# The gradient of wq in five separately placed pieces, and head groups of four whose out and dx products spread over 25 ticks

## The chip, the core and the metric

The kernel runs on one core of one Trainium2 chip. The metric is device time in microseconds (us) of one execution. The engines named here are TensorE (PE in the profile: matrix products and transposes; PEld is its weight load), VectorE (DVE), ScalarE (ACT), GpSimd (POOL) and SyncE (SP), whose queue issues all DMA transfers. PSUM is the memory that TensorE writes to; VectorE and ScalarE copy from there to SBUF, and such a copy is what "empties a bank" means below.

## What is computed

Two attention blocks, A and B, with the same shapes and separate data, forward and backward. Each has 8 batches, 32 heads, 96 queries per batch of width 640, and 512 cached keys and values of width 128 per batch and head. Everything is bfloat16 in memory.

```python
q = (x @ wq).reshape(B, Sq, H, Dh).transpose(0, 2, 1, 3)
scores = jnp.einsum("bhqd,bhkd->bhqk", q, k_cache) * (Dh ** -0.5)
p = _softmax(scores, axis=-1)
o = jnp.einsum("bhqk,bhkd->bhqd", p, v_cache)
out = o.transpose(0, 2, 1, 3).reshape(B, Sq, H * Dh) @ wo
```

The kernel returns `out` of both blocks side by side and, for a given gradient of it, the gradients of x, k_cache, v_cache, wq and wo: dx, dk, dv, dwq and dwo.

## The kernel before

**Ticks.** The work is cut into small functions. Each is handed to an `Emitter` with a tick and a slot number, and `run` sorts them by tick, then slot, then order of arrival, and calls them. So the order of each engine's instructions is written out by these numbers. Instructions of S and the softmax (`c_s2a` to `c_s3b`) have a raised priority and stand somewhat earlier than their slot says: S is placed into the last products of the tick before. One tick is the time that one pair (head, batch) takes; a head has 8 ticks, a block 256, and head h begins at tick `c0t = tick0 + 8 h`.

**Per pair.** One tick holds the stages of nine neighbouring pairs: S (L298, one product of 512 columns), its row maximum `negm` on VectorE (L300), the exponential `E_sb` on ScalarE (L310, with a read of the accumulated sums), `rinv` on VectorE (L320), `P_sb` on GpSimd (L329), the transposes of P and of dS on TensorE (L365, L346), their copies `PT_sb` (ScalarE, L378) and `dST_sb` (VectorE, L348), the products O and dQ (L359, L340, both into `x_ps`) with their copy `OD` (ScalarE, L375), dV (L389) and dK (L432) with copies on ScalarE (L392, L435), dP and its row correction dl (L417, L419), and `dS_sb` on VectorE (L421).

**Per head**, in slots behind the pair's work:
- `pB`, tick -3 of the head: transposes of wo and wq of the head, copies `woT_h` (ScalarE) and `wqT_h` (VectorE).
- `pC`, ticks -2 to 0: QT and dOT in two widths, 512 and 256 columns (L243).
- `pD`, ticks 1 and 2: the same two transposed back, copies `dOnat_h` and `Qnat_h` on VectorE.
- `qA`, tick 18: O transposed, copy `Onat` on ScalarE; tick 17: dQ transposed, copy `dQnat` on VectorE.
- `qB`, ticks 19 and 20: dwo in two halves of 320 columns (L469), copies on ScalarE and VectorE.
- `qD`, for odd heads: dwq of the pair of heads in 5 chunks of 128 rows, each six products of 256 columns (L490). Two chunks share a PSUM bank at tick 18, two at tick 19, one at tick 21; the copies are on VectorE (L162). The pair's store follows one tick after the last.

**Per group of heads.** The sums over heads in out and dx are taken in groups, held in float32 accumulators in SBUF. Block A has groups of 5, 5, 5, 5, 4, 4, 4 heads, block B of 5, 5, 5, 5, 5, 5, 2. For each group, `gU` runs 24 pieces: out and dx, six row tiles each, once with 512 and once with 128 columns; every piece is one product per head of the group into one bank (L514). The first group's banks are emptied by ScalarE, the others are added to the accumulators by VectorE (L518, L520). With `cLg` the tick of the group's last pair, a group of five puts its 12 out pieces on ticks cLg+7 to cLg+15 and its 12 dx pieces on cLg+16 to cLg+24; many ticks get two pieces, and 22 of 40 none. A group of four in block A takes seven ticks for each half.

**Buffers.** All PSUM tiles come from one ring of eight banks (`bank`). `wqT_h` has a ring of seven, `OD` (O and dQ of a head, read by `gU`) seven slots, `dQnat`, `dwq_sb`, `Onat` and `dwo_sb` one buffer each. A new `wqT_h` waits until the last dx piece of the group that read the old one.

Of the kernel before, what the change touches and what calls it, by code (L numbers as in the profile page):

```python
# [45 lines left out]
HK = dict(pA=-10, pA2=-9, pB=-3, pC0=[-2, 0], pC1=[-1, 0], pD1=1, pD0=2, qA0=18, qA1=17, qB=[19, 20], qD=[(18, 0, 2), (19, 2, 4), (21, 4, 5)])  # L46
EV = dict(pB0="act", pB1="dve", pC00="act", pC01="act", pC10="act", pC11="dve", pD0="dve", pD1="dve", qA0="act", qA1="dve", qB0="act", qB1="dve", qD="dve", gU="act")
GSPREAD0 = 9
PRIO_OFF = 2000
GSPREAD1 = 9  # L50
SLOTS = dict(LOAD=0, S2A=5, S2B=5.5, S1=6, S8=10, S7=20, S5=30, S4=40, S6=50, S3A=52, S3B=53, S5B=54, HEAD=SL_HEAD, GRP=SL_GRP)


def build_block(tc, em, tick0, blk, x, kc, vc, wq, wo, g_all, out_all, dx, dk, dv, dwq, dwo, ident, ones, pools, HG=6, first=True, groups=None):
    nc = tc.nc
    B, Sq, D = x.shape
    _, H, Sk, Dh = kc.shape
# [147 lines left out]
    def pB(h):  # L205
        def f():
            st = HS[(blk, h)]
            woT_ps = bank([128, DC * 128], BF16, "woT_ps")
            for c in range(DC):
                nc.tensor.transpose(woT_ps[:, c * 128:(c + 1) * 128], st["wo_h"][:, c * 128:(c + 1) * 128], ident[:])  # L210
            woT_h = hd.tile([128, DC * 128], BF16, name="woT_h", bufs=1)
            evac(EV["pB0"], woT_h[:], woT_ps[:])
            st["woT_h"] = woT_h
            wqT_ps = bank([128, DC * 128], BF16, "wqT_ps")
            for c in range(DC):
                nc.tensor.transpose(wqT_ps[:, c * 128:(c + 1) * 128], st["wq_h"][:, c, :], ident[:])
            wqT_h = hst.tile([128, D], BF16, name="wqT_h")
            evac(EV["pB1"], wqT_h[:], wqT_ps[:])
            st["wqT_h"] = wqT_h
            st["slot"] = (blk * H + h) % OD.shape[2]  # L220
            st["OT_h"] = OD[:, 0, st["slot"]]
            st["dQT_h"] = OD[:, 1, st["slot"]]
            st["QT_h"] = hd.tile([128, T], BF16, name="QT_h")
            st["dOT_h"] = hd.tile([128, T], BF16, name="dOT_h")
        return f

    def pC(h, which, si):
        def f():
# [12 lines left out]
            q_ps = bank([128, w], F32, "q_ps")  # L241
            for c in range(DC):
                nc.tensor.matmul(q_ps[:], lhs(c), rhsT[:, c, t0:t0 + w], start=(c == 0), stop=(c == DC - 1))  # L243
            evac(EV["pC%d%d" % (which, si)], dst[:, t0:t0 + w], q_ps[:], sc)
        return f
# [314 lines left out]
    for g in range(NG):  # L560
        h0 = GH0[g]
        for hh in range(groups[g]):
            h = h0 + hh
            c0t = tick0 + h * B
            if not (first and h == 0):
                em.add(c0t + HK["pA"], SLOTS["LOAD"] + 1.7, pA(h))
                em.add(c0t + HK["pA2"], SLOTS["LOAD"] + 1.7, pA2(h))
            em.add(c0t + HK["pB"], SL_HEAD, pB(h))
            fh = first and h == 0
            p0, p1, d1, d0, late = HK["pC0"], HK["pC1"], HK["pD1"], HK["pD0"], 0  # L570
            if fh:
                p1, d1, d0, late = [3, 3], 3, 4, 7
            elif h == 0:
                p0, p1, d1, d0, late = [-2, 2], [0, 3], 3, 4, 7
            for si in range(NTS):
                em.add(c0t + p0[min(si, 1)], SL_HEAD, pC(h, 0, si))
                em.add(c0t + p1[min(si, 1)], SL_HEAD + late, pC(h, 1, si))
            em.add(c0t + d1, SL_HEAD + (8 if late else 0), pD(h, 1))
            em.add(c0t + d0, SL_HEAD, pD(h, 0))
            for b in range(B):  # L580
                ct = c0t + b
                if b % NB == 0:
                    em.add(tick0 - 12 if first and h == 0 and b == 0 else ct + OFF["ldk"], SLOTS["LOAD"], c_ld(h, b, "K", 7))
                    em.add(ct + OFF["ldv"], SLOTS["LOAD"], c_ld(h, b, "V", 6))
                    if not k_on_pe(h, b):
                        em.add(ct + OFF["kt"], SLOTS["LOAD"] + 1, c_xt(h, b, "KT", 4))
                    em.add(ct + OFF["vt"], SLOTS["LOAD"] + 1, c_xt(h, b, "VT", 4))
                if k_on_pe(h, b):
                    em.add(ct + 2, SLOTS["S1"], c_s1(h, b))
# [29 lines left out]
        if g == 0:  # L619
            em.add(cLg + OFF["s5"] - 2, SL_LOAD, setup_acc)  # L620
        subs = [(0, t, gi) for t in range(TT) for gi in range(len(gsplits))] + [(1, t, gi) for t in range(TT) for gi in range(len(gsplits))]
        n_out = TT * len(gsplits)
        for i, (which, t, gi) in enumerate(subs):
            if which == 0:
                tk = cLg + OFF["s5"] + 2 + (i * gs0) // n_out
            else:
                tk = cLg + OFF["s8"] + 2 + gs0 - 3 + ((i - n_out) * gs1) // n_out
            em.add(tk, SL_GRP, gU(g, which, t, gi))
# [126 lines left out]
```

## Time and profile before

| | |
|---|---|
| runs | 1643.6, 1643.09, 1642.14 us; median 1643.09 |
| profiled execution | 1643.09 us, of which the profile's span is 1641.3 |
| granted TensorE clock | 1.000 |
| TensorE matmul, busy | 1621.3 us (99%) |
| TensorE weight load, busy | 1289.1 us (79%) |
| ScalarE, busy | 1388.7 us (85%) |
| VectorE, busy | 1268.2 us (77%) |
| GpSimd, busy | 526.7 us (32%) |
| DMA | 454.96 MB, mean 277 GB/s |

A matmul's record lasts longer than its share of the array: records of neighbouring matmuls overlap. So the busy share of TensorE says little on its waits. What a matmul costs in a stream is the distance from its start to the next one's. A timeline row with "x4" is four such instructions, merged, with the start of the first; text in brackets is idle time of the engine before it and what ended that.

### The profile page before, as it was taken

The page shows a single profiled execution, that of the slowest core. Times are in us where ns is not written, and L with a number is a line of the kernel's source. Part 1 is how long each engine was busy: PE and PEld are TensorE (multiplying, and loading weights), DVE is VectorE, ACT ScalarE, POOL GpSimd, SP SyncE. Part 2 cuts the span into 40 slices and gives each one's busy share as a digit, 9 for nine tenths or more (in the row PEclk, how much of TensorE's full clock was granted, in tenths as well). Part 3 has the DMA queues.
Part 4 walks back from the last instruction along what each step waited for, and adds up shares of the span by engine and source line. Part 5 has one row for each costly group of instructions (what it writes and reads, how often), then busy time and mean ns, then how long its engine had stood idle before and what let it go on. Part 6 is the DMA issues. An engine that isn't in the chain of part 4 may idle for free.

```text
span 1641.3 us, 55280 instructions
## 1 busy us (share of the span) xinstructions
PE 1621.3 (99%) x21048; PEld 1289.1 (79%) x21048; DVE 1268.2 (77%) x2856; ACT 1388.7 (85%) x3518; POOL 526.7 (32%) x1034
## 2 busy tenths in 40 slices
PE   8999999999999999999999999999999999999999
PEld 7887787787787787877878877877877877877876
DVE  6886677778787787788878867878778778777777
ACT  7999897898798797988869998978977978987975
POOL 2333232333233232333323332323322322332332
PEclk9999999999999999999999999999999999999999
DMA  9999999999999999999999999999999999999994
GB/s 266 289 282 294 269 291 291 271 271 292 260 272 293 279 274 271 264 281 285 297 284 292 293 289 279 284 298 260 291 291 258 280 277 282 283 292 259 281 276 146
DMA packets 875626, 454.96 MB, mean 277 GB/s; under 512 B 548192, under 2 KB 875360, under 8 KB 875360
## 3 DMA queue, kind: packets, MB, share of 16 engines
q1 hardware_dynamic: 875360, 451.43, 112.4%
q8 instruction: 165, 2.70, 0.7%
q14 instruction: 101, 0.83, 0.1%
HBM read 161.09 MB, written 159.12 MB: 195 GB/s over the span
## 4 chain that ended last, share of the span: by engine, by line
PE 81%; ACT 10%; DVE 4%; issue 3%; DMA 2%; SPq 0%; POOL 0%; ACTq 0%; DVEq 0%; POOLq 0%
PE q_ps L243 13%; PE o_ps L514 12%; PE dwq_ps L490 6%; PE dP_ps L417 6%; PE dK_ps L432 6%; PE dV_ps L389 5%; PE S_ps L298 5%; PE dst_ps L346 5%; PE dwo_ps L469 4%; PE x_ps L365 4%; PE x_ps L359 4%; PE x_ps L340 4%; ACT E_sb L310 3%; ACT dK_sb L435 2%; PE n_ps L258 2%
## 5 line engine op out<-in xcount | busy, mean ns | idle before, releaser
L329 POOL TENSOR_SCALAR P_sb<-E_sb,rinv 96x512 bf16<-96x512 bf16 x512 | 352.5, 689 | 1087.9 <-DVE rinv L320 1053.6
L310 ACT ACTIVATE E_sb<-S_ps,negm 96x512 bf16<-96x512 f32 x512 | 354.8, 693 | 119.2 <-DVE negm L300 116.8
L421 DVE SCALAR_TENSOR_TENSOR dS_sb<-dP_ps,dl_ps,P_sb 96x512 bf16<-96x512 f32 x512 | 383.6, 749 | 48.9 <-PE dl_ps L419 40.2
L435 ACT ACTIVATE dK_sb<-dK_ps 128x512 bf16<-128x512 f32 x512 | 306.9, 599 | 97.5 <-PE dK_ps L432 96.5
L300 DVE TENSOR_REDUCE negm<-S_ps 96x1 f32<-96x512 f32 x512 | 347.7, 679 | 44.3 <-PE S_ps L298 42.1
L392 ACT ACTIVATE dV_sb<-dV_ps 128x512 bf16<-128x512 f32 x512 | 315.8, 617 | 0.0
L378 ACT ACTIVATE PT_sb<-x_ps 128x384 bf16<-128x384 bf16 x512 | 257.5, 503 | 0.0
L514 PEld LDWEIGHTS <-OD 128*128 128x128 bf16 x1536 | 135.7, 98 | 103.3 <-issue 1.3
L389 PE MATMUL dV_ps<-dOnat_h,P_sb 96*128 96x128 bf16 x2048 | 197.9, 219 | 0.6 <-DVE dOnat_h L160 0.6
L432 PE MATMUL dK_ps<-Qnat_h,dS_sb 96*128 96x128 bf16 x2048 | 197.8, 219 | 0.0
L417 PE MATMUL dP_ps<-VT,dOT_h 128*96 128x512 bf16 x512 | 195.4, 382 | 0.7
L298 PE MATMUL S_ps<-KT,QT_h 128*96 128x512 bf16 x488 | 184.7, 379 | 3.9 <-ACT E_sb L310 2.7
L407 POOL TENSOR_TENSOR prod<-OD,dOT_h 128x96 bf16<-128x96 bf16 x512 | 185.6, 362 | 8.8 <-ACT OD L375 8.2
L348 DVE COPY dST_sb<-dst_ps 128x384 bf16<-128x384 bf16 x512 | 177.2, 346 | 14.0 <-PE dst_ps L346 13.2
L320 DVE RECIPROCAL rinv<-rowsum 96x1 f32<-96x1 f32 x512 | 80.0, 156 | 138.8 <-ACT E_sb L310 134.8
L346 PE MATMUL dst_ps<-ident,dS_sb 96*128 96x96 bf16 x2048 | 171.8, 206 | 4.3 <-ACT PT_sb L378 3.6
L375 ACT ACTIVATE OD<-x_ps 128x192 bf16<-128x192 f32 (+1 forms) x515 | 172.5, 335 | 3.4 <-PE x_ps L340 3.4
L359 PE MATMUL x_ps<-PT_sb,V_sb 128*128 128x96 bf16 x2048 | 172.2, 206 | 0.5 <-ACT PT_sb L378 0.5
L365 PE MATMUL x_ps<-ident,P_sb 96*128 96x96 bf16 x2048 | 171.7, 205 | 0.6 <-POOL P_sb L329 0.3
L340 PE MATMUL x_ps<-dST_sb,K_sb 128*128 128x96 bf16 x2048 | 170.7, 206 | 0.0
L340 PEld LDWEIGHTS <-K_sb 128*128 128x128 bf16 x2048 | 133.7, 98 | 37.1
L514 PE MATMUL o_ps<-wo_h,OD 128*128 128x128 bf16 (+1 forms) x768 | 141.0, 299 | 0.0
(75 smaller groups left out, 3051.9 us busy)
## 6 DMA issues: line engine op xcount, KB each, us to landing
out_dram<-dV_sb SPq DMA_DIRECT2D x256, 256.0 KB, 3.9
out_dram<-dK_sb SPq DMA_DIRECT2D x256, 256.0 KB, 3.6
K_sb<-in_A_k_cache_dram SPq DMA_DIRECT2D x128, 256.0 KB, 4.1
V_sb<-in_A_v_cache_dram SPq DMA_DIRECT2D x128, 256.0 KB, 4.1
K_sb<-in_B_k_cache_dram SPq DMA_DIRECT2D x128, 256.0 KB, 4.2
V_sb<-in_B_v_cache_dram SPq DMA_DIRECT2D x128, 256.0 KB, 4.0
out_dram<-dwo_sb SPq DMA_DIRECT2D x64, 160.0 KB, 3.2
out_dram<-dwq_sb SPq DMA_DIRECT2D x32, 320.0 KB, 3.8
```

Of the source, the lines that this page charges most:

```text
L298: nc.tensor.matmul(S_ps[:], hs["QT_h"][:, tok], st["KT"], start=True, stop=True)
L300: nc.vector.tensor_reduce(negm[:], S_ps[:], axis=AX.X, op=ALU.max, negate=True)
L310: nc.scalar.activation(E_sb[:], st["S_ps"][:], ACT.Exp, bias=st["negm"][:], scale=1.0, accum_out=rowsum[:])
L329: pinned(nc.gpsimd.tensor_scalar(P_sb[:], st["E_sb"][:], st["rinv"][:], 0.0, op0=ALU.mult, op1=ALU.add))
L340: nc.tensor.matmul(dQT_ps, st["K_sb"][:, c, :], st["dST_sb"][:, c * Sq:(c + 1) * Sq], start=(c == 0), stop=(c == KC - 1))
L389: nc.tensor.matmul(dV_ps[:, c * 128:(c + 1) * 128], P_sb[:, c * 128:(c + 1) * 128], hs["dOnat_h"][:, b * 128:(b + 1) * 128], start=True, s ...
L392: nc.scalar.activation(SB[(blk, h, b // 2, "v")][:, b % 2], dV_ps[:], ACT.Identity, scale=1.0)
L417: nc.tensor.matmul(dP_ps[:], hs["dOT_h"][:, tok], st["VT"], start=True, stop=True)
L421: nc.vector.scalar_tensor_tensor(dS_sb[:], dP_ps[:], dl_ps[:, 0:1], st["P_sb"][:], op0=ALU.subtract, op1=ALU.mult)
L432: nc.tensor.matmul(dK_ps[:, c * 128:(c + 1) * 128], dS_sb[:, c * 128:(c + 1) * 128], hs["Qnat_h"][:, b * 128:(b + 1) * 128], start=True, s ...
L435: nc.scalar.activation(SB[(blk, h, b // 2, "k")][:, b % 2], dK_ps[:], ACT.Identity, scale=1.0)
L514: nc.tensor.matmul(o_ps[:], src[:, t * 128:(t + 1) * 128], rhs, start=(hh == 0), stop=(hh == groups[g] - 1))
```

## The change

Four edits go together.

1. `Emitter.add` takes an estimate of the work's TensorE and ScalarE time in ns and keeps a load per tick, TensorE's minus 0.8 of ScalarE's. The calls for pB, pC, pD, qA, qB, gU and the K transposes of the first heads pass such numbers; the pair's own stages pass none.
2. `qD` of every odd head but the block's last is cut into five pieces of one chunk each. They are placed after everything else has been entered: each goes to the tick with the lowest load among ticks 18 to 29 of the odd head, at most two per tick; two in the same tick are emitted as one call with one bank. The last pair of heads of each block keeps the old ticks and pieces.
3. `qA` of dQ moves for even heads from tick 17 to tick 21, behind the other head work of its tick. Odd heads keep tick 17.
4. Block A has eight groups of 4, block B groups of 5, 5, 4, 4, 4, 4, 4, 2. A group of four puts its 12 out pieces on ticks cLg+7 to cLg+18, one each, and its 12 dx pieces on cLg+20 to cLg+31. Groups of five and two, and the last but one group of block B, keep nine, three and nine ticks for each half.

```diff
+HK = dict(pA=-10, ..., qA0=18, qA1=17, qA1e=21, qDw=(18, 29), qB=[19, 20], qD=[(18, 0, 2), (19, 2, 4), (21, 4, 5)])
...
-    def add(self, tick, slot, fn):
+    def add(self, tick, slot, fn, pe=0, act=0):
         self.items.append((tick, slot, self.n, fn))
         self.n += 1
+        self.load[tick] = self.load.get(tick, 0.0) + pe - ACT_SHARE * act
...
-            em.add(c0t + hk["qA1"], SL_HEAD, qA(h, 1))
-            for (k_, c_lo, c_hi) in hk["qD"]:
-                if c_lo < DC and h % 2 == 1:
-                    em.add(c0t + k_, SL_HEAD + 2, qD(h, c_lo, min(c_hi, DC)))
-            if h % 2 == 1:
+            em.add(c0t + (hk["qA1"] if h % 2 == 1 else HK["qA1e"]), SL_HEAD + (0 if h % 2 == 1 else 3), qA(h, 1), pe=335)
+            if h == H - 1:
+                for (k_, c_lo, c_hi) in hk["qD"]:
+                    em.add(c0t + k_, SL_HEAD + 2, qD(h, c_lo, min(c_hi, DC)), pe=655 * (c_hi - c_lo))
                 em.add(c0t + hk["qD"][-1][0] + 1, SLOTS["LOAD"] + 1.6, qD_st(h))
...
-        gs0 = max(3, (GSPREAD0 * groups[g]) // HG)
-        gs1 = max(3, (GSPREAD1 * groups[g]) // HG)
+        gs0, gs1 = {2: (3, 3), 4: (13, 13)}.get(groups[g], (9, 9))
...
+    for h in range(1, H - 1, 2):
+        c0t = tick0 + h * B
+        ticks = []
+        for _ in range(DC):
+            k_ = min((k for k in range(HK["qDw"][0], HK["qDw"][1] + 1) if ticks.count(k) < 2), key=lambda k: em.load.get(c0t + k, 0.0))
+            em.load[c0t + k_] = em.load.get(c0t + k_, 0.0) + 655
+            ticks.append(k_)
+        ticks.sort()
+        for k_ in sorted(set(ticks)):
+            em.add(c0t + k_, SL_HEAD + 2, qD(h, ticks.index(k_), ticks.index(k_) + ticks.count(k_)))
+        em.add(c0t + ticks[-1] + 1, SLOTS["LOAD"] + 1.6, qD_st(h))
...
-           ..., HG=5, ..., groupsA=None, groupsB=(5, 5, 5, 5, 5, 5, 2)):
+           ..., HG=5, ..., groupsA=(4,) * 8, groupsB=(5, 5, 4, 4, 4, 4, 4, 2)):
```

More of the change, by code (lines that the diff above doesn't have):

```diff
@@ L19, in __init__ @@
         self.n = 0
-    def add(self, tick, slot, fn):
+        self.load = {}
+    def add(self, tick, slot, fn, pe=0, act=0):
         self.items.append((tick, slot, self.n, fn))
         self.n += 1
+        self.load[tick] = self.load.get(tick, 0.0) + pe - ACT_SHARE * act
     def run(self):
@@ L45 @@
 OFF = dict(ldk=-5, ldv=-4, kt=-3, vt=0, s2=3, s3=3, s4=4, s5=5, s6=6, s7=7, s8=8)
-HK = dict(pA=-10, pA2=-9, pB=-3, pC0=[-2, 0], pC1=[-1, 0], pD1=1, pD0=2, qA0=18, qA1=17, qB=[19, 20], qD=[(18, 0, 2), (19, 2, 4), (21, 4, 5)])
+HK = dict(pA=-10, pA2=-9, pB=-3, pC0=[-2, 0], pC1=[-1, 0], pD1=1, pD0=2, qA0=18, qA1=17, qA1e=21, qDw=(18, 29), qB=[19, 20], qD=[(18, 0, 2), (19, 2, 4), (21, 4, 5)])
 EV = dict(pB0="act", pB1="dve", pC00="act", pC01="act", pC10="act", pC11="dve", pD0="dve", pD1="dve", qA0="act", qA1="dve", qB0="act", qB1="dve", qD="dve", gU="act")
 GSPREAD0 = 9
+ACT_SHARE = 0.8
 PRIO_OFF = 2000
@@ L567, in build_block @@
                 em.add(c0t + HK["pA2"], SLOTS["LOAD"] + 1.7, pA2(h))
-            em.add(c0t + HK["pB"], SL_HEAD, pB(h))
+            em.add(c0t + HK["pB"], SL_HEAD, pB(h), pe=558, act=713)
             fh = first and h == 0
@@ L575, in build_block @@
             for si in range(NTS):
[L576 to L579, printed above, removed]
+                em.add(c0t + p0[min(si, 1)], SL_HEAD, pC(h, 0, si), pe=1090 if si == 0 else 546, act=522 if si == 0 else 420)
+                em.add(c0t + p1[min(si, 1)], SL_HEAD + late, pC(h, 1, si), pe=1090 if si == 0 else 546, act=621 if si == 0 else 0)
+            em.add(c0t + d1, SL_HEAD + (8 if late else 0), pD(h, 1), pe=446)
+            em.add(c0t + d0, SL_HEAD, pD(h, 0), pe=446)
             for b in range(B):
@@ L588, in build_block @@
                 if k_on_pe(h, b):
-                    em.add(ct + 2, SLOTS["S1"], c_s1(h, b))
+                    em.add(ct + 2, SLOTS["S1"], c_s1(h, b), pe=223)
                 em.add(ct + OFF["s2"], SLOTS["S2A"], c_s2a(h, b))
@@ L603, in build_block @@
             hk = HK if first or h < H - 1 else dict(HK, qA0=13, qB=[14, 15], qA1=16, qD=[(19, 0, 2), (19, 2, 4), (19, 4, 5)])
-            em.add(c0t + hk["qA0"], SL_HEAD, qA(h, 0))
+            em.add(c0t + hk["qA0"], SL_HEAD, qA(h, 0), pe=335, act=820)
             for di in range(len(wsplits)):
-                em.add(c0t + hk["qB"][di], SL_HEAD + 1, qB(h, di))
+                em.add(c0t + hk["qB"][di], SL_HEAD + 1, qB(h, di), pe=815, act=443 if di == 0 else 0)
             em.add(c0t + hk["qB"][-1] + 1, SLOTS["LOAD"] + 1.6, qB_st(h))
-            em.add(c0t + hk["qA1"], SL_HEAD, qA(h, 1))
-            for (k_, c_lo, c_hi) in hk["qD"]:
-                if c_lo < DC and h % 2 == 1:
-                    em.add(c0t + k_, SL_HEAD + 2, qD(h, c_lo, min(c_hi, DC)))
-            if h % 2 == 1:
+            em.add(c0t + (hk["qA1"] if h % 2 == 1 else HK["qA1e"]), SL_HEAD + (0 if h % 2 == 1 else 3), qA(h, 1), pe=335)
+            if h == H - 1:
+                for (k_, c_lo, c_hi) in hk["qD"]:
+                    em.add(c0t + k_, SL_HEAD + 2, qD(h, c_lo, min(c_hi, DC)), pe=655 * (c_hi - c_lo))
                 em.add(c0t + hk["qD"][-1][0] + 1, SLOTS["LOAD"] + 1.6, qD_st(h))
         cLg = tick0 + (h0 + groups[g] - 1) * B + B - 1
-        gs0 = max(3, (GSPREAD0 * groups[g]) // HG)
-        gs1 = max(3, (GSPREAD1 * groups[g]) // HG)
+        gs0, gs1 = {2: (3, 3), 4: (13, 13)}.get(groups[g], (9, 9))
         if not first and g == NG - 2:
@@ L627, in build_block @@
                 tk = cLg + OFF["s8"] + 2 + gs0 - 3 + ((i - n_out) * gs1) // n_out
-            em.add(tk, SL_GRP, gU(g, which, t, gi))
+            em.add(tk, SL_GRP, gU(g, which, t, gi), pe=groups[g] * gsplits[gi][1] / 2.4, act=440 if g == 0 else 0)
             if g == NG - 1 and gi == len(gsplits) - 1:
                 em.add(tk + 1, SLOTS["LOAD"] + 1.6, gU_st(which, t))
+    for h in range(1, H - 1, 2):
[9 more added lines that the diff above has]
+        em.add(c0t + ticks[-1] + 1, SLOTS["LOAD"] + 1.6, qD_st(h))
     pools["c_s45"] = c_s45
```

2 lines of the change are left out of this document (1 added, 1 removed).

## The prediction

> **What bounds the kernel now.** I read the profile page first, then the matmuls in order of time, then ScalarE's and VectorE's rows in the same stretches.
>
> ```profile
> span 1641.3 us, 55280 instructions
> PE 1621.3 (99%) x21048; PEld 1289.1 (79%) x21048; DVE 1268.2 (77%) x2856; ACT 1388.7 (85%) x3518; POOL 526.7 (32%) x1034
> PE 81%; ACT 10%; DVE 4%; issue 3%; DMA 2%; SPq 0%; POOL 0%; ACTq 0%; DVEq 0%; POOLq 0%
> ```
>
> TensorE carries the run, but its 99% hides waits, since a matmul's record reaches into the next one's. Starts show them. The timeline of TensorE (start, duration, line, operation; in brackets a wait) has a light head:
>
> ```profile
> 23.50 0.34 PE L346 MATMUL dst_ps<-ident,dS_sb 96*128 96x96 bf16 x4
> ...
> 94.60 0.60 PE L243 MATMUL q_ps<-gT,woT_h 128*128 128x256 bf16 x4
> 95.04 0.33 PE L340 MATMUL x_ps<-dST_sb,K_sb 128*128 128x96 bf16 x4
> 95.21 0.34 PE L346 MATMUL dst_ps<-ident,dS_sb 96*128 96x96 bf16 x4
> 95.38 0.39 PE L432 MATMUL dK_ps<-Qnat_h,dS_sb 96*128 96x128 bf16 x4
> 95.61 0.34 PE L359 MATMUL x_ps<-PT_sb,V_sb 128*128 128x96 bf16 x4
> ...
> 96.17 0.38 PE L417 MATMUL dP_ps<-VT,dOT_h 128*96 128x512 bf16 x1
> 96.39 0.17 PE L419 MATMUL dl_ps<-ones,prod 128*96 128x1 bf16 x1
> ...
> 97.58 0.34 PE L346 MATMUL dst_ps<-ident,dS_sb 96*128 96x96 bf16 x4
> ...
> 100.15 0.34 PE L346 MATMUL dst_ps<-ident,dS_sb 96*128 96x96 bf16 x4
> ...
> 101.82 0.38 PE L298 MATMUL S_ps<-KT,QT_h 128*96 128x512 bf16 x1 [0.16 <-ACT E_sb L310]
> ...
> 102.88 0.34 PE L346 MATMUL dst_ps<-ident,dS_sb 96*128 96x96 bf16 x4
> ...
> 105.29 0.34 PE L346 MATMUL dst_ps<-ident,dS_sb 96*128 96x96 bf16 x4
> ...
> 107.27 0.33 PE L340 MATMUL x_ps<-dST_sb,K_sb 128*128 128x96 bf16 x4
> 107.77 0.33 PE L346 MATMUL dst_ps<-ident,dS_sb 96*128 96x96 bf16 x4 [0.17 <-ACT PT_sb L378]
> ...
> 1623.44 0.34 PE L346 MATMUL dst_ps<-ident,dS_sb 96*128 96x96 bf16 x4
> ```
>
> Unhindered, four matmuls of 96 columns start 0.17 us apart, four of 128 columns 0.23, one of 512 columns 0.22, four of 256 columns 0.44 (320 columns in proportion). One tick runs from a dst group to the next; there are 512 dst groups, the first at 23.50 and the last at 1623.44, so 511 ticks of 3.13 us on average. Priced by those distances, the matmuls between them need 3.06 us per tick. So all waits together are about 34 us: more than that the change can't win between these rows.
>
> Where are they? The ticks at 95.21 and 97.58 hold the same matmuls (nat and n transposes), yet last 2.37 and 2.57: 0.20 lost. Those at 100.15 and 102.88 both hold one dwo half: 2.73 against 2.41: 0.32 lost. At 107.27 the x group starts, dst should follow 0.17 later and follows after 0.50: 0.33 lost. ScalarE's timeline gives the reason:
>
> ```profile
> 99.80 0.60 ACT L392 ACTIVATE dV_sb<-dV_ps 128x512 bf16<-128x512 f32 x1
> 100.28 0.82 ACT L157 ACTIVATE Onat<-nat_ps 128x768 bf16<-128x768 bf16 x1
> 100.97 0.70 ACT L310 ACTIVATE E_sb<-S_ps,negm 96x512 bf16<-96x512 f32 x1
> ...
> 103.17 0.48 ACT L157 ACTIVATE dwo_sb<-dwo_ps 128x320 bf16<-128x320 f32 x1
> 103.48 0.74 ACT L310 ACTIVATE E_sb<-S_ps,negm 96x512 bf16<-96x512 f32 x1
> ```
>
> ScalarE needs 2.20 us for the six instructions of every tick (100.97 to 103.17), plus 0.69 for Onat and 0.31 for dwo. Two such ticks cost it 5.40 us, TensorE 2.37 + 2.41 = 4.78. In light ticks ScalarE is the bound, while TensorE leads it elsewhere. In the whole trace 18, 18 and 21 ticks have these three contents with neither dwq nor out/dx in them, and lose 0.20, 0.32 and 0.33 each with little scatter: 3.6 + 5.7 + 6.9 = 16.2 us.
>
> The second kind of wait sits in the heaviest ticks, where two out/dx pieces meet. VectorE and TensorE around one:
>
> ```profile
> 298.41 0.38 PE L417 MATMUL dP_ps<-VT,dOT_h 128*96 128x512 bf16 x1
> 298.86 0.75 DVE L421 SCALAR_TENSOR_TENSOR dS_sb<-dP_ps,dl_ps,P_sb 96x512 bf16<-96x512 f32 x1 [0.22 <-PE dl_ps L419]
> 299.54 0.54 DVE L160 COPY dQnat<-nat_ps 128x768 bf16<-128x768 bf16 x1
> 300.00 0.68 DVE L300 TENSOR_REDUCE negm<-S_ps 96x1 f32<-96x512 f32 x1
> 300.10 0.34 PE L346 MATMUL dst_ps<-ident,dS_sb 96*128 96x96 bf16 x4
> 300.60 0.68 DVE L160 COPY dOnat_h<-n_ps 96x1024 bf16<-96x1024 bf16 x1
> 301.33 0.12 PEld L417 LDWEIGHTS <-dOT_h 128*96 128x96 bf16 x1 [0.28 <-DVE dOnat_h L160]
> 304.27 0.34 PE L346 MATMUL dst_ps<-ident,dS_sb 96*128 96x96 bf16 x4
> ```
>
> dQnat (qA) and dOnat (pD) fall on VectorE back to back and dP waits for them. The tick lasts 4.17 us for 3.75 of matmuls: 0.42 lost. Eight ticks are like it; eight at pB's place lose 0.24 and nine one tick later 0.12: 3.4 + 1.9 + 1.1 = 6.4 us.
>
> **The change part by part.** *Placing.* TensorE's instructions stay the same 21048; only their order changes, and the built order follows the tick numbers. Priced as above, the mean tick stays 3.06 us, the ticks under 2.5 us fall from 141 to 45, those over 4.0 from 52 to 5. Of the three light contents (18, 18, 21) there remain 2, 7 and 0, and the tick ahead of six of the seven now has a dwq piece (0.66 us more), over the 0.62 by which ScalarE fell behind. I keep 0.7 us of the 16.2: gain 15.5. In the stretches of four-head groups the lightest head needs TensorE 23.3 us in its eight ticks against ScalarE's 20.4 (8 x 2.20, and 2.80 of head copies).
>
> *Groups of four.* With one out or dx piece per tick, ticks that hold a wide and a narrow piece fall from 90 to 18. Block B's first two groups still have five heads; the first empties through ScalarE, so one set of double ticks stays (0.42 + 0.24 + 0.12 = 0.8). Gain 6.4 - 0.8 = 5.6.
>
> *qA of even heads four ticks later* takes dQnat out of pD's tick for half the heads. It is in those 5.6 already. dQnat has one buffer, but the last dwq piece stands ahead of the next even head's qA in TensorE's order, so no wait is added.
>
> *More copies.* Sixteen groups instead of fourteen: 24 wide and 24 narrow adds more. dwq goes from 64 copies of 512 and 32 of 256 columns to 15 and 130.
>
> ```profile
> L162 DVE TENSOR_SCALAR dwq_sb<-dwq_ps 128x512 bf16<-128x512 f32 x64 | 44.3, 692 | 40.0 <-PE dwq_ps L490 40.0
> L518 DVE TENSOR_TENSOR out_acc<-o_ps,out_acc 128x512 f32<-128x512 f32 x60 | 41.4, 690 | 20.9 <-PE o_ps L514 20.7
> L518 DVE TENSOR_TENSOR out_acc<-o_ps,out_acc 128x128 f32<-128x128 f32 x60 | 16.6, 277 | 0.0
> L162 DVE TENSOR_SCALAR dwq_sb<-dwq_ps 128x256 bf16<-128x256 f32 x32 | 13.3, 416 | 3.9 <-PE dwq_ps L490 3.9
> L298 PE MATMUL S_ps<-KT,QT_h 128*96 128x512 bf16 x488 | 184.7, 379 | 3.9 <-ACT E_sb L310 2.7 <-DMA KT<-K_sb 0.8
> ```
>
> 24 x (0.690 + 0.277) + 15 x 0.692 + 130 x 0.416 - 44.3 - 13.3 = 30 us more on VectorE, taking the out row for dx too. VectorE goes from 77% to about 80%, under TensorE's matmuls, so I cost it at nothing on average; uncovered it would cost up to those 30. [...]
>
> *Bank waits.* PSUM is one ring of eight banks, and the change moves who follows whom. In the built order, S takes over dP's bank after only 1.02 to 1.14 us of matmuls in 35 ticks (never under 1.29 before). The bank is free when dS, which reads dP, has ended. In the fence above that is at 299.61, 0.98 after dP's last column (298.41 + 0.22). The latest dS of the steady part is this, behind a rinv that waits for a late ScalarE:
>
> ```profile
> 70.11 0.38 PE L417 MATMUL dP_ps<-VT,dOT_h 128*96 128x512 bf16 x1
> ...
> 70.93 0.16 DVE L320 RECIPROCAL rinv<-rowsum 96x1 f32<-96x1 f32 x1 [1.01 <-ACT E_sb L310]
> ...
> 71.01 0.75 DVE L421 SCALAR_TENSOR_TENSOR dS_sb<-dP_ps,dl_ps,P_sb 96x512 bf16<-96x512 f32 x1
> ```
>
> It ends 1.43 after dP's last column. So each place costs from 0 to 0.41 us, 0 to 14 in all; ScalarE is less late after the change, so the first row is nearer, and I take 0.1: 3.5 us. In 13 ticks of odd heads VectorE's instructions (3.26 us) match TensorE's (3.25), with dQnat, dOnat and a wide add together: 0 to 0.42 each by the row above, I take 0.1: 1.3. wqT's copy still waits for the group's last dx piece, holding one bank for 9 and 1 ticks of 32 (10 and 2 of 40 before): no difference.
>
> *Stores.* The 32 dwq stores move with the pieces past other entries of SyncE's queue, none added. TensorE's S waits 0.8 us in all for a transposed K, so nothing is near its due time: 0, at most those few tenths.
>
> **Sum.** -15.5 - 5.6 + 3.5 + 1.3 = -16.3. A further 2 us stand in bare ticks beside the light ones (about 0.05 each in some 30 that vanish) and in light ticks at the seam of the blocks; I add 1.5: -17.8. The profiled execution took 1643.09 (1641.3 of span and 1.8 around it), which is also the median of the three. Forecast 1625.3 us.
>
> **Rivals.** *VectorE bursts eat half.* If wide adds in front of dS, dQnat and dOnat push VectorE late in most of the 48 ticks above, at 0.25 each: 12 instead of 4.8, so 1632.5. For it: VectorE at 80% and the 0.42 above; against it: those had two pieces in a tick.
>
> *Slower: banks.* S takes dP's bank at 35 places. If dS there ended late enough that S lost over 0.63 us each, the 22 us won would be gone; at 0.85 it is 30 lost: 1651. Against it: the latest dS above gives 0.41. [...]
>
> *No change.* If the transposes and loads paced the ticks, evening them out would shift waits onto DMA: 1643. Against it: 0.8 us of such waits.
>
> **How the numbers follow.** Forecast with its own spread of 1616 to 1630: 0.64. VectorE bursts, 1630 to 1639: 0.21. No change: 0.05. Slower by banks: 0.10. Range 1616 to 1639: below, all 24 us and a little more won with no new wait; above, the bounds of the bank waits nearly used up. A measurement tells about 0.2% (3.3 us) from nothing. Faster 0.85, same 0.05, slower 0.10.
>
> **What would show it.** Right: the light ticks' brackets naming E_sb and PT_sb gone, ScalarE and VectorE waiting longer for TensorE, the first-to-last dst stretch near 1582 us. Wrong: S or dP with waits on dS, dOnat or an add repeating every four heads (the bank steps), or waits for KT and VT (the cover by DMA lead).

## The result

Runs of the changed kernel: 1631.55, 1628.68, 1628.85 and 1630.87 us, median 1629.86, against 1642.8 us for the kernel before on the same chip. The ratio is 0.9921, with a 95% interval from 0.9909 to 0.9933: 12.9 us or 0.8% faster. The forecast was 1625.3 us; the range and the direction held. The profiled execution is the one of 1631.55 us, the slowest of the four. In the experiments below, one execution of placing alone (1806.64 us) and two of the kernel before beside it ran at a granted clock of 0.69 to 0.85 and are in no median or ratio.

The page of the changed kernel: span; busy time, share and count of each engine; shares of the chain of work that ended last; and two of its groups (busy time, mean ns of one, idle time before them and what ended it).

```profile
span 1629.8 us, 55028 instructions
PE 1603.9 (98%) x20851; PEld 1283.2 (79%) x21048; DVE 1299.2 (80%) x2953; ACT 1397.9 (86%) x3518; POOL 526.4 (32%) x1034
PE 91%; DVE 4%; ACT 2%; issue 2%; DMA 1%; POOL 0%; SPq 0%; DVEq 0%; ACTq 0%; POOLq 0%
L313 ACT ACTIVATE E_sb<-S_ps,negm 96x512 bf16<-96x512 f32 x512 | 351.2, 686 | 149.7 <-DVE negm L303 144.9
L303 DVE TENSOR_REDUCE negm<-S_ps 96x1 f32<-96x512 f32 x512 | 348.4, 681 | 76.0 <-PE S_ps L301 74.7
```

The sign that the prediction gave for being right is there. Two rows of TensorE's waits in the kernel before (total us, times, longest) have gone; in the changed kernel E_sb and PT_sb end three single waits of TensorE, of 0.2 us each. The two rows were:

```profile
PE dst_ps L346 <- ACT PT_sb L378: 3.6, 21, 0.2
PE S_ps L298 <- ACT E_sb L310: 2.7, 17, 0.2
```

ScalarE's share of the chain fell from 10% to 2%, and TensorE's rose from 81% to 91%. VectorE is busy 31.0 us longer. Line numbers of the helpers are higher by 3. Some 200 matmul records are missing from this trace, so the matmuls of a tick are taken from the built order.

Here are the first and the last dst group:

```profile
23.41 0.34 PE L349 MATMUL dst_ps<-ident,dS_sb 96*128 96x96 bf16 x4
...
1612.18 0.29 PE L349 MATMUL dst_ps<-ident,dS_sb 96*128 96x96 bf16 x3
```

They are 1588.77 us apart, 11.2 less than before. Priced as in the prediction, the waits of the 511 ticks fell from 34.4 to 22.9 us. What is new among the 22.9 stands at three kinds of place.

**One stop of 3.5 us.** Tick 292, at 925.6 us, lasts 6.61 us for 3.07 of matmuls, and the next one loses 0.72. The timelines of VectorE, TensorE and SyncE's queue at that place (start, duration; in brackets the wait):

```profile
928.99 0.42 DVE L165 TENSOR_SCALAR dwq_sb<-dwq_ps 128x256 bf16<-128x256 f32 x1 [2.86 <-DMA out_dram<-dwq_sb]
...
929.47 0.97 PE L472 MATMUL dwo_ps<-g_nat,Onat 128*128 128x320 bf16 x6 [2.50 <-DVE dwq_sb L165]
...
924.96 0.43 SPq L501 DMA_DIRECT2D out_dram<-dwq_sb  x1
```

The dwq store of heads 32 and 33 was due when its last copy had ended, at 911.9. It was issued at 924.96, 13.1 us later: in the trace SyncE's queue has loads, transposes and stores ahead of it from 911.9 on, with no gap over 0.1 us between them. The first dwq copy of the next pair stands only five ticks behind that last piece, and `dwq_sb` has one buffer. So the copy waits for the store, and everything on VectorE behind it waits too.

Busy time and granted clock (PEclk) in three stretches from there:

```profile
928.00:930.36 2.36, 0.89 (x7) 0.66 (x7) 1.37 (x4) 0.56 (x2) 0.51 (x1) 1.00 1.64 281
930.36:933.77 3.41, 3.41 (x30) 2.79 (x29) 1.57 (x5) 1.77 (x4) 0.96 (x3) 0.50 0.84 235
933.77:936.00 2.23, 2.23 (x32) 1.81 (x30) 1.63 (x3) 1.43 (x5) 0.59 (x2) 1.00 1.17 344
```

The wait of 2.50 us ends at 929.47; from 930.36 to 933.77 us, for 3.41 us, the granted clock is 0.50, and 1.00 before and behind it. Half of 3.41 us is 0.1% of 1629.8, so by estimate one such stretch takes the mean clock of a run to 0.999. Two of the four runs have that (1631.55 and 1630.87 us), the other two have 1.000 (1628.68 and 1628.85 us). So, by the same estimate, the half clock is not in every run.

**Odd heads' ticks.** Ticks 67, 99, 131 and on (ten of them) lose 0.33 us each, and ticks 83, 115, 147 and on (also ten) 0.28: 6.1 us. Here are VectorE and then TensorE at tick 99:

```profile
317.46 0.75 DVE L424 SCALAR_TENSOR_TENSOR dS_sb<-dP_ps,dl_ps,P_sb 96x512 bf16<-96x512 f32 x1 [0.28 <-PE dl_ps L422]
318.13 0.54 DVE L163 COPY dQnat<-nat_ps 128x768 bf16<-128x768 bf16 x1
318.59 0.68 DVE L303 TENSOR_REDUCE negm<-S_ps 96x1 f32<-96x512 f32 x1
319.19 0.68 DVE L163 COPY dOnat_h<-n_ps 96x1024 bf16<-96x1024 bf16 x1
...
319.60 0.38 PE L420 MATMUL dP_ps<-VT,dOT_h 128*96 128x512 bf16 x1
320.02 0.18 PE L422 MATMUL dl_ps<-ones,prod 128*96 128x1 bf16 x1
320.19 0.49 PE L458 MATMUL nat_ps<-ident,OD 128*128 128x128 bf16 x6
```

dl follows dP by 0.42 instead of 0.22 and takes over the bank of `n_ps`, which is free only when dOnat's copy ends at 319.87. In ticks 83, 115 and on it is another bank: in the built order dl stands there 1.35 us of matmuls behind a narrow out or dx piece, whose bank VectorE's addition has to free.

**S behind dP's bank.** S loses 0.17 us at places with 1.03 us of matmuls between them, 0.135 at 1.02, and nothing at 1.14: 3.7 us in all.

So 4.3 + 6.1 + 3.7 = 14.1 us of waits are new by these three causes. With a net fall of 11.5, some 25.6 us of the old ones are gone.

### The profile page after: what moved, and what is told of

The parts are those of the page before. It is cut to its first block, busy times and chain, and to the rows that moved or that the text cites. A ratio compares the mean times of both kernels' runs of the same rounds, so it can differ in the third digit from the quotient of the medians.

```text
span 1629.8 us, 55028 instructions
## 1 busy us (share of the span) xinstructions
PE 1603.9 (98%) x20851; PEld 1283.2 (79%) x21048; DVE 1299.2 (80%) x2953; ACT 1397.9 (86%) x3518; POOL 526.4 (32%) x1034
## 4 chain that ended last, share of the span: by engine, by line
PE 91%; DVE 4%; ACT 2%; issue 2%; DMA 1%; POOL 0%; SPq 0%; DVEq 0%; ACTq 0%; POOLq 0%
PE q_ps L246 13%; PE o_ps L517 11%; PE dK_ps L435 7%; PE S_ps L301 7%; PE dV_ps L392 6%; PE dwo_ps L472 6%; PE dwq_ps L493 6%; PE dP_ps L420 6%; PE dst_ps L349 5%; PE x_ps L368 5%; PE x_ps L343 5%; PE x_ps L362 5%; PE n_ps L261 3%; PE nat_ps L458 3%; DVE dS_sb L424 1%
## 5 line engine op out<-in xcount | busy, mean ns | idle before, releaser
L313 ACT ACTIVATE E_sb<-S_ps,negm 96x512 bf16<-96x512 f32 x512 | 351.2, 686 | 149.7 <-DVE negm L303 144.9
L438 ACT ACTIVATE dK_sb<-dK_ps 128x512 bf16<-128x512 f32 x512 | 301.3, 589 | 51.7 <-PE dK_ps L435 50.5
L395 ACT ACTIVATE dV_sb<-dV_ps 128x512 bf16<-128x512 f32 x512 | 310.3, 606 | 0.0
L381 ACT ACTIVATE PT_sb<-x_ps 128x384 bf16<-128x384 bf16 x512 | 252.3, 493 | 0.0
L517 PEld LDWEIGHTS <-OD 128*128 128x128 bf16 x1536 | 140.0, 98 | 103.9 <-issue 3.9
L378 ACT ACTIVATE OD<-x_ps 128x192 bf16<-128x192 f32 (+1 forms) x515 | 167.3, 325 | 3.2 <-PE x_ps L343 3.2
L517 PE MATMUL o_ps<-wo_h,OD 128*128 128x128 bf16 (+1 forms) x706 | 148.7, 292 | 3.3
```

What stands on the lines that cost most here:

```text
L313: nc.scalar.activation(E_sb[:], st["S_ps"][:], ACT.Exp, bias=st["negm"][:], scale=1.0, accum_out=rowsum[:])
L395: nc.scalar.activation(SB[(blk, h, b // 2, "v")][:, b % 2], dV_ps[:], ACT.Identity, scale=1.0)
L438: nc.scalar.activation(SB[(blk, h, b // 2, "k")][:, b % 2], dK_ps[:], ACT.Identity, scale=1.0)
L517: nc.tensor.matmul(o_ps[:], src[:, t * 128:(t + 1) * 128], rhs, start=(hh == 0), stop=(hh == groups[g] - 1))
```

## The experiments

Ratios are to the kernel before on the same chip, and a gain or loss in us is taken from the ratios. "The changed kernel" has 0.9921 from its four runs above; it was not run again beside the experiments.

**Is it the store? Four runs on one chip.** First, the last dwq piece of each block's first pair comes earlier.

```diff
-min((k for k in range(HK["qDw"][0], HK["qDw"][1] + 1) ...
+min((k for k in range(HK["qDw"][0], HK["qDw"][1] + (0 if h == 1 else 1)) ...
```

> Against the changed kernel, only the first pair of each block gives its last dwq piece one tick earlier (tick 28 of the head, not 29), so that between the last piece of heads 32 and 33 and the first copy of the next pair lie seven ticks and not five. Store theory: the 2.5 us in which TensorE stands still at 929.5 us, the 2.9 us wait of the dwq copy for its store and the stretch at half clock behind it are gone; the time is about 1626 us, 3 to 4.3 below the changed kernel's 1629.9. Rival, that the store only shows a lateness of the loads which would cost the same elsewhere: the wait turns up at another pair or as a wait for KT, VT or K_sb, and the time stays at about 1629.5.

Measured: 1630.76 us, ratio 0.9918 (0.9905 to 0.9931): no gain that can be told. In the profiled run no copy waits for its store any more, and the dst stretch is 2.7 us shorter. But its first dst comes at 25.55 us, 2.1 later than in the changed kernel, behind a wait for x and a stretch at half clock (0.50) from 8.15 to 11.56 us, in a part that the edit doesn't touch. And tick 293 now loses 1.17 us, in which S waits 1.0 for the transposed K (`KT`). So the theory of the store is near for the stop (2.7 us where it had 3 to 4.3), and the rival is partly right: a wait for loads has taken the store's place.

The second run moves dQnat of odd heads.

```diff
-HK = dict(..., qA1=17, ...
+HK = dict(..., qA1=16, ...
```

> Against the changed kernel, only the dQnat transpose and copy of odd heads come one tick earlier (tick 16 and not 17), away from dOnat's copy. Burst theory: the 20 ticks of odd heads that lose 0.33 and 0.28 us each (67, 99, 131 and on; 83, 115, 147 and on) lose little, about 5 to 6 us less: 1624 us with the wait for the store still there. Rival, that these ticks lose by the order in which the PSUM banks come round, whatever VectorE copies there: the losses stay or move by a tick, and the time stays within 1 us of 1629.9.

Measured: 1626.13 us, ratio 0.9895 (0.9882 to 0.9908), 4.3 us better than the changed kernel's ratio. Ticks 67, 99 and on fall from 3.3 to 1.3 us in sum, ticks 83, 115 and on from 2.8 to 1.8. So half of the 6.1 us came from dQnat ahead of dOnat; the other half stays. Another 2.6 us went at ticks 284 to 296, where the wait for the store fell to 1.2 us (the granted clock of the profiled run is 1.000); this the theory had not named.

> Both edits together. If the two theories hold and do not overlap, their gains add: about 1620.5 us, 9 below the changed kernel. If one of them only moves the loss, about 1625. If both only move it, 1629.

Measured, with both edits: 1624.91 us, ratio 0.9888 (0.9873 to 0.9902), the best of all runs. The waits of the 511 ticks are 15.9 us, the dst stretch 1581.8. The gains do not add: it is 1.2 us below the second run, which the intervals don't tell apart. S still waits 0.63 us for KT at 928 us.

The fourth run gives `dwq_sb` a second buffer.

```diff
-st["dwq_sb"] = hd.tile([128, DC, 256], BF16, name="dwq_sb", bufs=1)
+st["dwq_sb"] = hd.tile([128, DC, 256], BF16, name="dwq_sb", bufs=2)
-stp=P(name="stp", bufs=5),
+stp=P(name="stp", bufs=4),
```

> The changed kernel's order, with two buffers for dwq_sb instead of one, paid for by the ring of small tiles going from five to four. Store theory: the copy no longer waits for the store of the pair before, whatever SyncE's queue does; about 1626 us, as with the earlier last piece, with the store still issued about 13 us after its copy. Rival as there: about 1629.5. If the shorter ring bites, waits on its tiles show in VectorE's or ScalarE's rows and the time is above 1630.

Measured: 1632.29 us, ratio 0.9927 (0.9914 to 0.994); its six runs spread from 1628.22 to 1635.42. Its waits of TensorE (total, times, longest) and the longest one in the timeline:

```profile
PE S_ps L301 <- DMA KT<-K_sb: 4.2, 2, 3.4
...
934.32 0.61 PE L301 MATMUL S_ps<-KT,QT_h 128*96 128x512 bf16 x1 [3.40 <-DMA KT<-K_sb]
```

With the store out of the way S stops for K's transpose within 5 us of the old place, and longer. The shorter ring of small tiles is not the reason by the trace: the loads and stores that use it are issued at most 2 us later than in the changed kernel. So it isn't the store alone; the transposes of K are late there. From the end of KT's issue to the S that reads it there are 11 to 14 us on average over most of the kernel before (a KT lands 4.6 us after the start of its issue, the median of the trace). But between 900 and 940 us that lead falls to its lowest in every kernel run: 3.5 us in the kernel before and in the changed one, 4.3 with the first edit, 4.5 with the first two, 2.6 here. At its narrowest KT lands less than 0.1 us ahead of S in all fourteen kernels (0.05 in the kernel before, at 921.36, and in the changed one, at 913.43). The kernel before already ran without reserve at this place, and paid 0.8 us in all; the longer of its two waits:

```profile
921.41 0.42 PE L298 MATMUL S_ps<-KT,QT_h 128*96 128x512 bf16 x1 [0.58 <-DMA KT<-K_sb]
```

**Is it SyncE's queue or the transfers?**

```diff
-pinned(nc.sync.dma_start(dwo[...
+pinned(nc.gpsimd.dma_start(dwo[...       # the same for dwq, and for out and dx
```

> The changed kernel with the 110 stores of dwo, dwq and out/dx issued by GpSimd's queue and no longer by SyncE's. Queue theory (SyncE's queue of loads, transposes and stores is unbroken from 820 to 930 us and runs late as a whole, the dwq store only being the first to show it): 110 entries of 0.45 to 0.8 us leave it, K's transpose lies more than 8 us ahead of S at 900 to 930 us where it was 3.5, and the dwq store is issued within 2 us of its copy: the 3.5 and 0.7 us of ticks 292 and 293 and the stretch at half clock go, 1625 to 1626.5 us. Rival, that the transfers themselves are late, whichever queue issues them: a wait for the store or for KT stays near 925 us and the time is 1629 or above. A third way: the issues or their waits hold up P_sb on GpSimd, which shows as waits of VectorE's dS and TensorE's dV for P_sb, and the time is above 1632.

Measured: 1632.31 us, ratio 0.9926 (0.9914 to 0.9939). The dwq store is now issued 0.3 us after its copy, and tick 292 loses nothing. But KT's lead is still only 4.3 us at 926 us:

```profile
930.73 0.42 PE L301 MATMUL S_ps<-KT,QT_h 128*96 128x512 bf16 x1 [0.66 <-DMA KT<-K_sb]
```

The trace has 120 entries on GpSimd (64 of dwo, 32 of dwq, 24 of out and dx), not 110. The queue theory's number for the lead (over 8) is wrong: taking them off SyncE brings the loads forward by less than 1 us. Between 820 and 930 us SyncE issues 108 entries where it issued 123, with no gap over 0.9 us between them, since each takes longer: a transpose 1.67 us on average for 1.59, the others 0.59 for 0.53. The loads of K and V land 4.9 us after the start of their issue for 4.4. That speaks for transfers that are late whoever issues them, as the rival had it. (DMA's digit on the pages can't show it: it is 9 nearly from start to end.) What stands there besides, in the changed kernel from 820 to 905 us, are 12 stores of block A's out and dx and 6 loads of block B's x and gradient. They are 3.9 MB, some 14 us at the 279 GB/s of the run by an estimate, and the lead falls by about that much, from 17 us to 3.5. No run moves them, so that they are the reason is not shown. The third way is out: no row of dS or dV waits for P_sb.

The dst stretch is 2.9 us shorter than the changed kernel's, but the end comes 3.4 us later after the last dst (21.0 for 17.6 us), with out and dx's stores and GpSimd's own additions taking turns:

```profile
1621.04 1.28 POOL L544 TENSOR_TENSOR gT<-xT,dx_acc 128x512 bf16<-128x512 f32 x1
1622.24 0.56 POOL L554 DMA_DIRECT2D out_dram<-gT  x1
1622.83 0.47 POOL L544 TENSOR_TENSOR gT<-xT,dx_acc 128x128 bf16<-128x128 f32 x1
```

The same on the best kernel, with dwo and dwq stores alone on GpSimd:

> The changed kernel with odd dQnat at tick 16 and the earlier last piece, and the 96 stores of dwo and dwq issued by GpSimd, those of out and dx again by SyncE. If the 3.4 us longer end in the run with all 110 on GpSimd came from the out and dx stores behind its additions, the end is again 17.6 us after the last dst; the 0.8 us that tick 293 still loses go or shrink: ratio about 0.988, 0.5 to 1 us below the same kernel with SyncE's stores. If the transfers themselves are late at 925 us, K's transpose is still only 4 to 5 us ahead of S there and the time is unchanged.

Measured: 1627.36 us, ratio 0.9902 (0.9887 to 0.9918), no gain over 0.9888. KT's lead is 4.1 us at 918, S waits 1.33 us, and the end takes 19.4 us, not 17.6: the expectation that it comes back was wrong.

**Which half of the change pays?** Each was put alone on the kernel before. Placing alone keeps before's groups:

```diff
-        gs0, gs1 = {2: (3, 3), 4: (13, 13)}.get(groups[g], (9, 9))
+        gs0 = max(3, (GSPREAD0 * groups[g]) // HG)
+        gs1 = max(3, (GSPREAD1 * groups[g]) // HG)
-           groupsA=(4,) * 8, groupsB=(5, 5, 4, 4, 4, 4, 4, 2)):
+           groupsA=None, groupsB=(5, 5, 5, 5, 5, 5, 2)):
```

> The kernel before with the five dwq pieces placed in the lightest ticks and qA of even heads four ticks later, but with its own groups of five heads and their spreads. Light-tick theory: of the three light contents (18, 18 and 21 ticks) there remain 1, 25 and 0, half of them behind a tick that now holds a dwq piece; the 16.2 us become 2 to 6; the 6.4 us in double ticks stay, and 1 to 3 us of waits for dwq stores may come. So 8 to 13 us below the kernel before. Rival, that groups of four are what counts: less than 5 us below it.

Measured: 1631.02 us, ratio 0.9917 (0.9903 to 0.993), the whole gain. The waits of the 511 ticks are 20.3 us, among them again a stop at the same place:

```profile
PE dwo_ps L472 <- DVE dwq_sb L165: 2.3, 2, 2.1
...
PE S_ps L301 <- DMA KT<-K_sb: 1.2, 1, 1.2
```

Groups of four alone is the reverse diff on the kernel before.

> The kernel before with groups of four heads, whose out and dx pieces spread over 13 and 13 ticks, and dwq in its three pieces at their old ticks. Light-tick theory: the light contents stay (28, 16 and 16 ticks, about 16 us), the double ticks fall from 90 to 18 and give 5.6 us back, S follows dP's bank closely at 12 places (about 1 us): 3 to 6 us below the kernel before, so that the two halves nearly add up to the 13 us of the whole. Rival, that the 30 us more of VectorE eat it: no gain, or slower.

Measured: 1646.6 us, ratio 1.0015 (1.0006 to 1.0024): 2.5 us slower. The waits of the 511 ticks are 37.9 us, 3.6 more than before, although most double ticks are gone: the odd heads' ticks named above, with the one ahead of 83, 115 and on, lose 7.7 us where the kernel before lost 2.4, and ten ticks with nothing but nat and n transposes (75, 107 and on) lose 0.43 each, where the kernel before lost 0.19 in such ticks. One of these ten, TensorE and VectorE:

```profile
352.14 0.38 PE L417 MATMUL dP_ps<-VT,dOT_h 128*96 128x512 bf16 x1
352.55 0.17 PE L419 MATMUL dl_ps<-ones,prod 128*96 128x1 bf16 x1
...
350.66 0.54 DVE L160 COPY dQnat<-nat_ps 128x768 bf16<-128x768 bf16 x1
351.13 0.68 DVE L300 TENSOR_REDUCE negm<-S_ps 96x1 f32<-96x512 f32 x1
351.73 0.68 DVE L160 COPY dOnat_h<-n_ps 96x1024 bf16<-96x1024 bf16 x1
```

It is the same row of events as in the changed kernel, with no dwq piece near. So this loss belongs to the groups of four. In the built order of the kernel before, dl takes over the bank of `nat_ps` in most such ticks, 2.02 us of matmuls after the last write to it. With one out or dx piece per tick the ring has moved by a place, and dl gets the bank of `n_ps`, 1.79 us after, which dOnat's copy has to free.

Are groups of four worth something once dQnat is moved? Placing alone, with both small edits of the best kernel:

> Placing alone with groups of five (as in the run of dwq alone), and beside it the two edits that helped the changed kernel: odd heads' dQnat at tick 16, and the first pair's last dwq piece one tick earlier. If groups of four are worth something once dQnat is out of dOnat's tick, this stays 3 to 5 us above the changed kernel with the same two edits (ratio 0.9888 to the kernel before): 0.991 to 0.992. If groups of four are worth nothing, the ratio is 0.989 here too.

Measured: 1631.86 us, ratio 0.9923 (0.9909 to 0.9937), as the first theory says. But the reason is another one. Of the 7.2 us of waits that it has over the best kernel, 6.0 stand in ticks 284 to 296:

```profile
914.12 0.42 PE L301 MATMUL S_ps<-KT,QT_h 128*96 128x512 bf16 x1 [1.97 <-DMA KT<-K_sb]
...
926.15 0.42 PE L301 MATMUL S_ps<-KT,QT_h 128*96 128x512 bf16 x1 [0.52 <-DMA KT<-K_sb]
...
933.92 0.66 PE L301 MATMUL S_ps<-KT,QT_h 128*96 128x512 bf16 x1 [2.23 <-DMA KT<-K_sb]
```

The rest of the run differs by 1.2 us, in favour of groups of four. Without the two edits the same comparison outside these ticks, the changed kernel against placing alone, was 2.0 us against them. Why the loads are later here with groups of five stays open.

The last one on dQnat's place puts it at tick 15 (and that of block B's last head, which has a tick of its own, from 16 to 15):

> The changed kernel with the earlier last piece and odd dQnat at tick 15 and not 16. The built order has the same 24 places where S follows dP's bank closely, so if these set what is left in the odd heads' ticks (0.12 and 0.18 us each), they stay and so does the time: 1624.9. If the copy of dQnat still does it at 16, they go: 2 to 3 us less.

Measured: 1635.86 us, ratio 0.9954 (0.9942 to 0.9967), 10.9 us worse than at 16. The odd heads' ticks keep exactly their 0.12 and 0.18 us, as the first theory says; but ticks 64, 80, 96 and on lose 0.21 or 0.47 each (10.7 us over all ticks at that place in the head, 0.7 with dQnat at 16), and the waits of TensorE and of its weight load show why:

```profile
PEld L458 <- ACT OD L378: 13.9, 30, 0.6
...
PE nat_ps L458 <- ACT OD L378: 4.2, 14, 0.3
```

The transpose needs the head's last dQ, whose copy has only just ended. Of the three ticks tried, 16 is the best.

**Why do light ticks lose?** Two kernels without any placing. The first:

```diff
-EV = dict(..., qA0="act", ...
+EV = dict(..., qA0="dve", ...
```

> The kernel before with only the copy of Onat (64 x 0.69 us) moved from ScalarE to VectorE; order and PSUM ring unchanged. If ScalarE is the bound in the light ticks, their waits for E_sb and PT_sb go without any placing: 8 to 13 us less, or somewhat fewer where the copy makes VectorE late instead. Rival, that the ring of eight banks is too short there and the engine that empties it does not matter: within 2 us of the kernel before.

Measured: 1642.01 us, ratio 0.9987 (0.9978 to 0.9996): 2.1 us less. The nat tick still loses 0.19, the first dwo tick 0.18 (0.32 before), the wo/wq tick 0.32. The other leaves the copy on ScalarE and shortens it (from 819 to 286 ns on average); five of the six row tiles of O are left out of dwo:

```diff
+                if which == 0:
+                    nt = 1
                 evac(EV["qA%d" % which], dst[:, t0:t0 + nt, :], ...
-                nc.tensor.matmul(w_ps[:], Onat[:, t, :], ...
+                nc.tensor.matmul(w_ps[:], Onat[:, 0, :], ...
```

> The kernel before, with Onat's copy on ScalarE cut from 768 to 128 columns (0.69 to about 0.25 us, 64 times) and dwo's matmuls all reading that one column block, so that their number, size and order stay; dwo is then not the reference's. Nothing is put on VectorE instead. Theory that ScalarE's work is the bound in the light ticks: the dwo tick at 100.15 and the like (0.32) loses almost nothing, the wo/wq tick at 105.29 and the like (0.33) at most 0.15, since ScalarE comes to it earlier, and the nat tick at 97.58 (0.20), which lies ahead of the copy, stays: 7 to 10 us below the kernel before. Rival, that the loop from S over negm, E, rinv and P through all engines is as long as the tick, whoever is busy in it: the losses are those of the run with Onat on VectorE (0.19, 0.18, 0.32), about 2 us below the kernel before.

Measured: 1638.64 us, ratio 0.9969 (0.9957 to 0.998), 5.1 us less. The three contents lose 0.19, 0.04 and 0.33. So in the dwo tick ScalarE's work is the bound. Moved to VectorE, the same copy gives back only half of that tick's loss. The built order isn't quite that of the kernel before there, although the expectation took it as unchanged: dwo's first product takes over the bank of S. That is free when E's read of the sums ends, at 101.47, and E itself waited for negm and not for ScalarE:

```profile
99.92 0.68 DVE L300 TENSOR_REDUCE negm<-S_ps 96x1 f32<-96x512 f32 x1
100.69 0.68 ACT L310 ACTIVATE E_sb<-S_ps,negm 96x512 bf16<-96x512 f32 x1 [0.31 <-DVE negm L300]
...
101.31 0.16 PE L419 MATMUL dl_ps<-ones,prod 128*96 128x1 bf16 x1
101.52 0.43 PE L469 MATMUL dwo_ps<-g_nat,Onat 128*128 128x320 bf16 x2
```

The nat tick lies ahead of the shortened copy, so the run doesn't test it. For the wo/wq tick neither theory has the number: its loss does not move at all. ScalarE, VectorE and TensorE there, in the run with the short copy:

```profile
103.43 0.70 ACT L310 ACTIVATE E_sb<-S_ps,negm 96x512 bf16<-96x512 f32 x1
...
104.26 0.16 DVE L320 RECIPROCAL rinv<-rowsum 96x1 f32<-96x1 f32 x1 [0.73 <-ACT E_sb L310]
104.34 0.75 DVE L421 SCALAR_TENSOR_TENSOR dS_sb<-dP_ps,dl_ps,P_sb 96x512 bf16<-96x512 f32 x1
105.01 0.68 DVE L300 TENSOR_REDUCE negm<-S_ps 96x1 f32<-96x512 f32 x1
...
105.78 0.68 ACT L310 ACTIVATE E_sb<-S_ps,negm 96x512 bf16<-96x512 f32 x1
...
107.69 0.33 PE L346 MATMUL dst_ps<-ident,dS_sb 96*128 96x96 bf16 x4 [0.17 <-ACT PT_sb L378]
```

From one E to the next the work runs through both engines in a ring: E 0.83 with its sums, rinv 0.08, dS 0.67, negm 0.77, then E again, 2.35 us after the first. The wo/wq tick has 2.16 us of matmuls, less than one turn. VectorE has idle time in it, and ScalarE a little: its six instructions need 2.20 us, and the turn takes 2.35. That the turn sets 0.19 of the 0.33 us is read from these rows, not shown by a run of its own. It can't be the reason in the nat tick, whose 2.37 us of matmuls are longer than the turn; what costs 0.20 there stays open.

## Why the prediction was right or wrong, step by step

- *Placing, 15.5 us.* Right in size: placing alone took 14.1 us of waits away, with a new stop of up to 3.8 us already inside. The cause given, that ScalarE is the bound in light ticks, is shown for the dwo tick alone (5.7 of the 16.2 us): 0.32 to 0.04 when its copy is cut. In the wo/wq tick the rows speak for the turn E, rinv, dS, negm, and in the nat tick the cause is open. A tick that gets a dwq piece (0.66 us) outlasts any of them, so the size came out right with the mechanism right for a third of it; that is in part luck.
- *Groups of four, 5.6 us.* Wrong as a gain of this change. Alone they cost 2.5 us, and with the placing the ratio goes from 0.9917 to 0.9921, which can't be told apart. With the two small edits in both it goes from 0.9923 to 0.9888, but 6.0 of the 7.2 us of waits between them stand at ticks 284 to 296. The doubled ticks were priced; what a spread over more ticks does to the ring of banks in the ticks of dQnat and dOnat was priced at 1.3 us and is the loss.
- *qA of even heads, no wait.* Right; no row names dQnat's buffer. The odd heads, which keep tick 17, were the ones to look at.
- *More copies, 30 us hidden.* 31.0 measured, and hidden on average. The "VectorE bursts" rival named the right mechanism for half of the loss at the odd heads, which is the next point.
- *Bank waits.* S behind dP's bank: 3.5 forecast, 3.7 measured. The term "13 ticks of odd heads" was mis-sized: 1.3 us forecast, 6.1 measured in 20 ticks. The row it was priced from had its lower end taken, although the 0.42 us of its upper end came from the same three copies. dQnat's place explains half of it: some 3 us stay with dQnat at tick 16 and at 15 alike, and their cause stays open. They repeat every four heads, the sign of being wrong that the prediction had named.
- *Stores, "nothing is near its due time: 0".* This step failed: 4.3 us in two ticks of the profiled run, with a stretch at half clock in it that no term allowed for. It read a small sum of waits (0.8 us for KT) as a reserve. The lead of the loads, which was in the trace of before, would have shown 3.5 us at 912 us where it is 11 to 14 on average elsewhere; and the distance from the last piece to the next pair's first copy, five ticks, was in the built order.
- *No change, paced by DMA*, was given 0.05. As a bound of the whole it is wrong, but in one stretch of some 40 us KT comes just in time or late in every kernel here, at up to 6 us (placing alone with dQnat at 16, over the best kernel).

The sum: 25.6 us gone where 22.6 were forecast, and 14.1 us new where 4.8 were. The two errors, 3.0 and 9.3 us, have opposite signs. The forecast lay 4.6 us below the measured median.

## What to carry to other kernels

A small total of waits for an engine or a queue says that it was in time, not by how much: before work or stores are moved past it, list the lead of each transfer over its use along the whole run, and look at the minimum. When pieces are spread out of crowded ticks, price the ticks that they are spread into, above all those where two long copies already follow each other on the engine that must take them. And before one engine is called the bound of a short tick, add up the turn through all engines from one E to the next: here it was longer than what any engine alone needed in the wo/wq tick, and less work for ScalarE two ticks ahead gave nothing back.

## What was not expected of the hardware

How long TensorE waited did not by itself decide whether the half clock followed. Here are stretches of 3.41 us, as long as the half clock of the changed kernel lasted (length, busy time of TensorE and its count, then of PEld, VectorE, ScalarE and GpSimd; the last three numbers are clock, DMA share and GB/s). First placing alone with dQnat at 16, counted back in steps of that length from the fall of its clock at 933.49 us:

```profile
909.60:913.01 3.41, 2.55 (x38) 1.95 (x35) 3.09 (x7) 3.41 (x10) 1.61 (x3) 1.00 1.16 123
913.01:916.43 3.42, 2.25 (x29) 1.72 (x31) 1.04 (x2) 1.63 (x4) 0.39 (x2) 1.00 1.16 343
...
930.08:933.49 3.41, 1.61 (x28) 1.29 (x26) 1.78 (x5) 2.33 (x6) 1.02 (x2) 1.00 1.17 293
933.49:936.90 3.41, 2.98 (x20) 2.12 (x21) 1.48 (x4) 0.77 (x2) 0.00 (x0) 0.50 1.25 229
```

then placing alone, in three stretches of other lengths, and the run with the earlier last piece, near its start:

```profile
927.00:929.10 2.10, 0.05 (x2) 0.00 (x0) 0.43 (x2) 1.64 (x5) 0.00 (x0) 1.00 1.15 351
929.10:932.00 2.90, 2.85 (x38) 2.45 (x38) 2.31 (x6) 1.17 (x4) 1.02 (x2) 1.00 1.15 353
932.00:935.00 3.00, 3.00 (x45) 2.48 (x43) 2.50 (x7) 2.74 (x8) 1.10 (x3) 1.00 1.27 188
...
4.74:8.15 3.41, 1.47 (x23) 1.30 (x24) 0.98 (x2) 1.30 (x2) 0.00 (x0) 1.00 1.09 373
8.15:11.56 3.41, 3.19 (x23) 2.40 (x22) 0.98 (x2) 1.41 (x2) 0.00 (x0) 0.50 1.08 363
```

The wait of 1.97 us at 914.12 lies across two of these stretches, in which TensorE is busy 2.55 and 2.25 us, and the clock stays at 1.00. In placing alone, with its wait of 2.09 us, TensorE is busy for 0.05 of the 2.10 us up to 929.10, and the clock is 1.00 there and in the 5.90 us behind. From 4.74 to 8.15 us in the other run it is idle for 1.94 us in sum, less than either of these waits, and the clock is 0.50 for the 3.41 us that follow. Ahead of the fall at 933.49 TensorE has 1.61 us of work in 3.41, and in the changed kernel ahead of 930.36 0.89 in 2.36. What decides whether the clock falls is not shown by these rows.
